# Folding step 1 of an FFT-style convolution over the sign of j and running it as four 64x64 TensorE tiles

## The chip, the cores and the metric

The kernel runs on one core of one Trainium2 chip. The metric is device time of one execution in microseconds, as the median of several runs. The engines are named as in the profile: PE (TensorE matmul), PEld (TensorE weight load), DVE (VectorE), ACT (ScalarE), POOL (GpSimd) and SP (SyncE, which issues nearly all DMAs here).

## The reference

Two layers follow each other. The first is a long convolution with a gate: a filter is made from position embeddings, the product x*v of 4 sequences of 11456 tokens and 128 channels is convolved with it through an FFT of twice the length, and the result is multiplied by x. The second is a soft mixture of experts over the 45824 resulting tokens. The change touches the first layer only.

```python
h_filt = (np.maximum(pos_emb @ w1, 0.0) @ w2) * np.exp(-0.01 * pos)[:, None]
u = x * v
Uf = np.fft.rfft(u, n=2 * S, axis=1)
Hf = np.fft.rfft(h_filt, n=2 * S, axis=0)
y = np.fft.irfft(Uf * Hf[None], n=2 * S, axis=1)[:, :S, :]
attn = x * y
logits = attn @ phi          # then softmax over tokens and over slots, 8 experts of
                             # 128 -> 1024 -> 128, and a weighted sum back to tokens
```

## The kernel before, in words

The transform has length 111 x 197, and a token's place is written as 111 j + r, with 105 values of j (from -52 to 52) and 56 of r, so that a long FFT becomes four short matrix steps. All data is fp32. Channels are worked in 8 groups g of 16 channels, so 64 (batch, channel) pairs in a group, and these in 16 units u of four pairs.

- **p1_load** (lines 197 to 218) fetches one unit: the tile `x` (line 199) and the tile `v` (line 209) from the queue of SP, multiplies them on POOL (line 211; every third unit of group 0 on DVE), and folds over the sign of r: `sd` is x(r)+x(-r) and x(r)-x(-r), two DVE instructions (line 214) of 112x256 each. `x` and `v` come from the pool `ld` of 5 buffers, which the tiles `xi` (the gate's x, lines 264 to 266) share; in group 0, `v` lies in an unused region instead. `sd` comes from the pool `st` of 3 buffers.
- **p1** (lines 220 to 222, `first` at lines 122 to 135) is step 1, the sum over j: for each of two pairs of channels two matmuls with 105 rows (j), 128 columns (both signs of r) and 198 moving columns (cosines and sines). One PSUM tile of pool `psa` (4 buffers) holds a pair of channels. Three ACT instructions take it out to `T` (lines 130, 131, 135; in group 0 the third is one of DVE, line 133).
- **p2** (lines 224 to 241) is the sum over r (line 229), the multiplication by the filter on DVE (line 234) and the complex sums on POOL (lines 240 and 241), which write `T` again.
- **p3** (lines 243 to 256) is the first inverse sum: four matmuls (line 247) for two pairs, one ACT copy `ec` (line 251) and two DVE instructions into `E` (line 253). PSUM pool `psb` has 4 buffers.
- **p4** (lines 269 to 289) is the last inverse sum (line 277) and the gate on DVE (line 283), and **p4_out** stores the tile `xo` (lines 301 and 309).

After the filter has been made, the main loop (lines 314 to 366) runs over g. In it come two stages. In the *mixed stage* each unit u issues p1_load for unit u+2, two p3 of group g-1, and p1 of unit u. In the *p2/p4 stage* p2 of group g and p4 of group g-1 alternate. Group 0 has p1 without p3, and then p2 with the filter's last step. Behind the loop follows the mixture of experts.

The order on each engine is made by a scheduler from this program order and its own estimates; `inorder` pins an instruction to the program's order. POOL's products of x and v are pinned. The DVE folds are pinned in group 1 only, and the `E` additions of group 0's p3 also. Each engine works its queue strictly in order, and SP its DMA issues too, so an entry that waits holds back all that stands behind it. A buffer of a pool is given to a new tile when the old tile's last reader has been placed; the DMA that fills it waits for that reader.

The built program gives the places of the tiles. In the mixed stages of groups 2 to 7 `v` of a unit takes the place of `v` of the unit two earlier, from unit 2 on, and the last reader of that one is the product on POOL (line 211); `x` takes the place of `x` three units earlier.

Of the kernel before, what the change touches and what calls it, by code (L numbers as in the profile page):

```python
# [59 lines left out]
def conv_part(ctx, tc, cp, moe, xf, vf, xi, pos, w1, w2, win, t1x, t1h, wt, t3, t4, hs, scr):  # L60
    nc = tc.nc
    ld = ctx.enter_context(tc.tile_pool(name="ld", bufs=5))
    st = ctx.enter_context(tc.tile_pool(name="st", bufs=3))
# [57 lines left out]

    def first(src, tab, dst, shift):

        ps = psa.tile([128, 2, 2, J], F32, tag="psa", name=f"p1_{next(ids)}")
        for i in range(2):
            nc.tensor.matmul(ps[:, i].rearrange("p s k -> p (s k)"), lhsT=src(i), rhs=tab,  # L126
                             start=True, stop=True)
# [2 lines left out]
        nc.scalar.activation(to[0:RP], pq[0:RP], AF.Copy)  # L130
# [66 lines left out]
    def p1_load(g, u):  # L197
        xt = ld.tile([JP, 4, 2 * RP], F32, tag="ld", name=f"x_{g}_{u}")
        dma = nc.sync.dma_start(out=xt, in_=xf[g, u])
        if g == 0:  # L200
# [8 lines left out]
        nc.sync.dma_start(out=vt, in_=vf[g, u])
# [1 line left out]
        inorder(eng.tensor_tensor(out=xt, in0=xt, in1=vt, op=ALU.mult))  # L211
        sd = st.tile([JP, 4, 2 * RP], F32, tag="st", name=f"sd_{g}_{u}")
        for h, op in ((0, ALU.add), (RP, ALU.subtract)):
            add = nc.vector.tensor_tensor(out=sd[:, :, h : h + RP], in0=xt[:, :, 0:RP], in1=xt[:, :, RP:],  # L214
                                          op=op)
# [575 lines left out]

def _layout(x, v, pos_emb):
    p, b, m = _index(ORG)

    def fold(a):
        t = np.stack([_take(a, p), _take(a, b, True)], 1)
        t = t.reshape(B, 2, JT, R, G, CG).transpose(4, 0, 5, 2, 1, 3)
        pad = np.zeros((G, C // 4, JP, 4, 2, RP), a.dtype)
        pad[:, :, :JT, :, :, :R] = t.reshape(G, C // 4, 4, JT, 2, R).transpose(0, 1, 3, 2, 4, 5)
        return pad.reshape(G, C // 4, JP, 4, 2 * RP)  # L800

# [53 lines left out]
```

## Time and profile before

| | |
|---|---|
| runs | 1116.45, 1119.45, 1120.04 us |
| median | 1119.45 us |
| profiled execution, span | 1116.5 us |
| PE / PEld busy | 1044.0 / 973.1 us |
| DVE / POOL / ACT busy | 860.3 / 591.4 / 567.5 us |
| p1 of group 0 | 70.5 to 99.9 us of the span |
| mixed stages, groups 1 to 7 | about 50 us each; the one of group 3 from 251.5 to 303.7 us |
| p2/p4 stage behind that | 303.7 to 351 us |

The page gives the profiled execution as its span only, and the span is as long as the fastest of the three runs (1116.45 us), 2.95 us under the median. In the profile a kernel matmul of fp32 stands as two MATMUL and two LDWEIGHTS instructions. Busy time of PE is that of the union of overlapping instructions, each with a fill and drain of about 0.16 us, so an engine that is "busy" may still have room. Durations of DVE and ACT instructions also overlap the next one's start a little, so what one costs in a row of equal ones is read from the distance of their starts, or from a merged row of several.

### The profile page before, as it was taken

How to read it: one execution, taken by the hardware profiler on the slowest of the kernel's cores; microseconds unless marked ns; L12 is line 12 of the kernel's file. 1: busy time of each engine (PE TensorE's matmuls, PEld its weight loads, DVE VectorE, ACT ScalarE, POOL GpSimd, SP SyncE). 2: the span in 40 equal slices, each digit the busy share in tenths (PEclk: the TensorE clock that was granted, in tenths of full speed). 3: DMA queues.
4: the chain of work that ended last, by engine and by line, in shares of the span. 5: the costliest groups of instructions: out<-in, count | busy, mean ns of one | idle time of the engine just before them, and what ended most of it. 6: DMA issues, size and time to landing. Idle time of an engine off the chain costs nothing.

```text
span 1116.5 us, 26150 instructions
## 1 busy us (share of the span) xinstructions
PE 1044.0 (94%) x9360; PEld 973.1 (87%) x9360; DVE 860.3 (77%) x1774; ACT 567.5 (51%) x1441; POOL 591.4 (53%) x742
## 2 busy tenths in 40 slices
PE   6998989999999999999999999999999979997997
PEld 6987989998999999899999999999999966664775
DVE  5237669786898779788868977787798649997797
ACT  0678559306901850491086039307801228775697
POOL 6203764484377437545743755474374006776874
PEclk9999989999999999999999999999999999998999
DMA  9614767246534834572474458247546698773388
GB/s 289 209 59 154 268 218 212 87 128 192 163 110 138 234 96 128 168 219 80 136 220 123 124 158 230 86 128 198 158 124 220 167 276 244 213 212 98 155 352 337
DMA packets 129484, 198.49 MB, mean 178 GB/s; under 512 B 15926, under 2 KB 71537, under 8 KB 129356
## 3 DMA queue, kind: packets, MB, share of 16 engines
q1 hardware_dynamic: 129070, 196.65, 57.6%
q8 instruction: 76, 1.25, 0.5%
q14 instruction: 52, 0.43, 0.1%
q10 hardware_dynamic: 254, 0.11, 0.0%
q0 software_dynamic: 32, 0.07, 0.0%
HBM read 136.88 MB, written 59.90 MB: 176 GB/s over the span
## 4 chain that ended last, share of the span: by engine, by line
PE 45%; DVE 15%; issue 11%; ACT 6%; DMA 5%; POOL 3%; SPq 1%; ACTq 0%; DVEq 0%; POOLq 0%
PE p L277 13%; PE p L229 10%; PE p L126 8%; PE p L247 8%; DVE E L253 5%; DMA v<-in_vf_dram 4%; PE ct L713 2%; POOL x L211 2%; DVE xreg L424 2%; ACT T L130 2%; PE pt L483 1%; DVE sd L214 1%; DVE rd L503 1%; DVE xreg L729 1%; ACT ec L251 1%
## 5 line engine op out<-in xcount | busy, mean ns | idle before, releaser
L251 ACT ACTIVATE ec<-p 99x224 f32<-99x224 f32 x256 | 83.8, 356 | 392.6 <-issue 336.8
L253 DVE TENSOR_TENSOR E<-p,ec 99x224 f32<-99x224 f32 x512 | 222.2, 552 | 46.3 <-ACT ec L251 45.8
L240 POOL TENSOR_TENSOR T<-m,m 111x256 f32<-111x256 f32 (+1 forms) x200 | 145.7, 729 | 185.1 <-DVE m L234 183.7
L234 DVE TENSOR_TENSOR m<-p,T 111x512 f32<-111x512 f32 (+1 forms) x350 | 215.7, 677 | 22.9 <-issue 16.6
L247 PE MATMUL p<-tab,T 111*99 111x112 f32 x2048 | 221.8, 262 | 7.1 <-POOL T L240 3.0
L211 POOL TENSOR_TENSOR x<-x,v 112x512 f32<-112x512 f32 x112 | 144.5, 1291 | 154.4 <-DMA v<-in_vf_dram 135.8
L247 PEld LDWEIGHTS p<-tab,T 111*99 111x99 f32 x2048 | 214.9, 171 | 12.1 <-POOL T L240 3.2
L277 PE MATMUL p<-E,tab 99*105 99x128 f32 (+1 forms) x1792 | 214.0, 275 | 11.4 <-DVE E L253 11.4
L277 PEld LDWEIGHTS p<-E,tab 99*105 99x105 f32 x1792 | 204.1, 173 | 13.7 <-DVE E L253 11.3
L126 PE MATMUL p<-tab1x,sd 105*128 105x198 f32 x1024 | 200.5, 341 | 14.5 <-DVE sd L214 11.7
L229 PE MATMUL p<-T,W 128*111 128x128 f32 x1584 | 200.0, 278 | 1.1 <-DVE T L133 1.1
L229 PEld LDWEIGHTS p<-T,W 128*111 128x111 f32 x1584 | 188.3, 175 | 2.8 <-DVE T L133 1.3
L126 PEld LDWEIGHTS p<-tab1x,sd 105*128 105x128 f32 x1024 | 171.1, 194 | 21.7 <-DVE sd L214 11.4
L214 DVE TENSOR_TENSOR sd<-x 112x256 f32<-112x256 f32 x256 | 116.4, 496 | 64.5 <-POOL x L211 54.6
L241 POOL TENSOR_TENSOR T<-m,m 111x256 f32<-111x256 f32 (+1 forms) x200 | 145.8, 729 | 0.0
L130 ACT ACTIVATE T<-p 64x396 f32<-64x396 f32 x256 | 136.9, 535 | 11.7 <-PE p L126 7.9
L283 DVE TENSOR_TENSOR xo<-p,xi 105x256 f32<-105x256 f32 x224 | 84.0, 416 | 43.8 <-PE p L277 33.4
L131 ACT ACTIVATE T<-p 64x198 f32<-64x198 f32 x256 | 90.1, 352 | 3.0
L135 ACT ACTIVATE T<-p 64x198 f32<-64x198 f32 x224 | 74.2, 331 | 0.0
L531 POOL TENSOR_TENSOR E<-lt,mx 128x480 f32<-128x480 f32 (+1 forms) x24 | 24.6, 1025 | 70.6 <-PE pt L483 67.5
L717 ACT ACTIVATE cs<-ct 96x512 fp32r<-96x512 f32 x96 | 53.3, 567 | 10.4 <-PE ct L713 7.1
L713 PE MATMUL ct<-ident,c 128*96 128x128 f32 x358 | 55.3, 274 | 2.2 <-POOL c L693 1.4
(95 smaller groups left out, 1065.6 us busy)
## 6 DMA issues: line engine op xcount, KB each, us to landing
x<-in_xf_dram SPq DMA_DIRECT2D x128, 224.0 KB
v<-in_vf_dram SPq DMA_DIRECT2D x112, 224.0 KB
xi<-in_xi_dram SPq DMA_DIRECT2D x112, 224.0 KB
out_dram<-xreg SPq DMA_DIRECT2D x22, 960.0 KB
xreg<-scr SPq DMA_DIRECT2D x21, 960.0 KB
scr<-xo SPq DMA_DIRECT2D x104, 192.0 KB
hs<-E SPq DMA_DIRECT2D x12, 1024.0 KB
T<-hs SPq DMA_DIRECT2D x63, 176.0 KB
```

Source lines behind the costliest of these rows:

```text
L126: nc.tensor.matmul(ps[:, i].rearrange("p s k -> p (s k)"), lhsT=src(i), rhs=tab, start=True, stop=True)
L130: nc.scalar.activation(to[0:RP], pq[0:RP], AF.Copy)
L211: inorder(eng.tensor_tensor(out=xt, in0=xt, in1=vt, op=ALU.mult))
L214: add = nc.vector.tensor_tensor(out=sd[:, :, h : h + RP], in0=xt[:, :, 0:RP], in1=xt[:, :, RP:], op=op)
L229: nc.tensor.matmul(ps[:, i].rearrange("p b c -> p (b c)"), lhsT=W[:, k0 + i, :], rhs=Tf[:, :, k0 + i, :], start=True, stop=True)
L234: nc.vector.tensor_mul(m[:, :n].rearrange("p k s c i -> p k (s c i)").rearrange("p k (b c) -> p k b c", c=CG), ps[:, :n], h[:, :, CG * s : ...
L240: nc.gpsimd.tensor_tensor(out=Ty[:, 0], in0=ms[0][:, :n, 0], in1=ms[1][:, :n, 1], op=ALU.subtract)
L241: nc.gpsimd.tensor_tensor(out=Ty[:, 1], in0=ms[1][:, :n, 0], in1=ms[0][:, :n, 1], op=ALU.add)
L247: nc.tensor.matmul(ps[:, i, 2 * s : 2 * s + 2, :].rearrange("p q r -> p (q r)"), lhsT=T[0:N1, s, c // CG, c % CG // 2, :, i], rhs=tab3[:, ...
L251: nc.scalar.activation(ec, ps[:, :, 2:4, :], AF.Copy)
L253: add = nc.vector.tensor_tensor(out=E[:J, :, 2 * s : 2 * s + 2, c : c + 2].rearrange("p r q c -> p c q r"), in0=ps[:, :, 0:2, :], in1=ec, ...
L277: nc.tensor.matmul(ps[:, i, :n], lhsT=tab4[:, s, o : o + JT], rhs=E[:J, r, s : s + 2 * n - 1 : 2, :], start=(s == 0), stop=(s == 1))
```

## The change

**Step 1 itself.** The sums over j and -j are folded too. The host lays x and v out with the 53 values of |j| on 64 partitions, for two channels at a time (partitions 0 to 63 and 64 to 127), and with four quarters along the free axis: the signs of j and of r. The two halves of j are added and subtracted first (`m`, new line 215: two instructions of 128x224, written over the tile `v`; on POOL, except in group 0, where half of them are on DVE). Then the two signs of r are added and subtracted as before (`d`, new line 219: two DVE instructions of 128x224, written over the tile `x`, read from `v`). The sums meet cosines and the differences meet sines, so that each output needs 53 rows, 64 columns and 99 moving columns: 16 matmuls a unit (new line 130), which cycle through the four 64x64 quarters of the array, in place of 4 of 105 rows, 128 columns and 198 moving columns. The two PSUM tiles of a unit each hold two channels in the order in which `T` wants them, and one ACT instruction of 128x396 takes each out (new line 135) in place of three.

**Around it.** `sd` has no buffer of its own any more. `ld` has 7 buffers instead of 5. p1 runs for two units at a time, in odd u, with the loads of the next two units behind them. A unit's x is 256 KB instead of 224 KB (rows of 64 for 56 values of r); v stays at 224 KB. The table `tab1x` is 128x297 instead of 105x198.

```diff
-    ld = ctx.enter_context(tc.tile_pool(name="ld", bufs=5))
+    ld = ctx.enter_context(tc.tile_pool(name="ld", bufs=7))
...
-    def first(src, tab, dst, shift):
+    def first(g, u, sd):
-        ps = psa.tile([128, 2, 2, J], F32, tag="psa", name=f"p1_{next(ids)}")
+        ps = [psa.tile([128, 2, 2, J], F32, tag="psa", name=f"p1_{g}_{u}_{h}") for h in range(2)]
         for i in range(2):
-            nc.tensor.matmul(ps[:, i].rearrange("p s k -> p (s k)"), lhsT=src(i), rhs=tab,
-                             start=True, stop=True)
-        to = dst.rearrange("p s k c -> p s c k")
-        pq = ps.rearrange("p c s k -> p s c k")
-        nc.scalar.activation(to[0:RP], pq[0:RP], AF.Copy)
-        nc.scalar.activation(to[RP:128, 0], pq[RP:128, 1], AF.Copy)
-        if shift:
-            nc.vector.tensor_scalar_mul(to[RP:128, 1], pq[RP:128, 0], -1.0)
-        else:
-            nc.scalar.activation(to[RP:128, 1], pq[RP:128, 0], AF.Copy, scale=-1.0)
+            for s in range(2):
+                for h in range(2):
+                    js = slice(RP * h, RP * h + JH)
+                    for d in range(2):
+                        nc.tensor.matmul(ps[h][RP * d : RP * d + RP, i, s, :], lhsT=sd[js, i, s, d, :],
+                                         rhs=tab1x[js, J * (s + d) : J * (s + d + 1)],
+                                         start=True, stop=True, tile_position=(RP * h, RP * d))
+        for h in range(2):
+            dst = T[:, :, u // 4, 2 * (u % 4) + h]
+            nc.scalar.activation(dst, ps[h].rearrange("p c s k -> p s k c"), AF.Copy)
...
         nc.sync.dma_start(out=vt, in_=vf[g, u])
         eng = nc.vector if g == 0 and u % 3 == 2 else nc.gpsimd
-        inorder(eng.tensor_tensor(out=xt, in0=xt, in1=vt, op=ALU.mult))
-        sd = st.tile([JP, 4, 2 * RP], F32, tag="st", name=f"sd_{g}_{u}")
-        for h, op in ((0, ALU.add), (RP, ALU.subtract)):
-            add = nc.vector.tensor_tensor(out=sd[:, :, h : h + RP], in0=xt[:, :, 0:RP], in1=xt[:, :, RP:],
+        inorder(eng.tensor_tensor(out=xr, in0=xr, in1=vt, op=ALU.mult))
+        for m, op in ((0, ALU.add), (2, ALU.subtract)):
+            eng = nc.vector if g == 0 and (u + m // 2) % 2 else nc.gpsimd
+            inorder(eng.tensor_tensor(out=vt[:, :, m : m + 2], in0=xr[:, :, 0:2], in1=xr[:, :, 2:4], op=op))
+        sd = xt.rearrange("p c (s d) r -> p c s d r", s=2)
+        vq = vt.rearrange("p c (s q) r -> p c s q r", s=2)
+        for d, op in ((0, ALU.add), (1, ALU.subtract)):
+            add = nc.vector.tensor_tensor(out=sd[:, :, :, d, :R], in0=vq[:, :, :, 0], in1=vq[:, :, :, 1],
                                           op=op)
...
-                if u + 2 < NU:
-                    sds[u + 2] = p1_load(g, u + 2)
                 if g > 0:
                     p3(g - 1, 4 * u)
                     p3(g - 1, 4 * u + 2)
-                p1(g, u, sds.pop(u))
+                if u % 2:
+                    p1(g, u - 1, sds.pop(u - 1))
+                    p1(g, u, sds.pop(u))
+                    for w in (u + 1, u + 2):
+                        if w < NU:
+                            sds[w] = p1_load(g, w)
```

**What the change does to the order.** First the queue of DVE in the mixed stage of group 3, before, from the fold of unit 10 on. `sd_3_10` is the fold of group 3's unit 10, and `E` the addition of two pairs of p3, as two instructions:

```order
L214 TENSOR_TENSOR sd_3_10_4057<-x_3_10_4052 112x4x64 x2
L253 TENSOR_TENSOR E_86<-p3_2_32_4060,ec_2_32_4065 99x2x2x56 x2
L253 TENSOR_TENSOR E_86<-p3_2_34_4069,ec_2_34_4074 99x2x2x56 x2
L214 TENSOR_TENSOR sd_3_11_4096<-x_3_11_4091 112x4x64 x2
L253 TENSOR_TENSOR E_86<-p3_2_36_4099,ec_2_36_4104 99x2x2x56 x2
L253 TENSOR_TENSOR E_86<-p3_2_38_4108,ec_2_38_4113 99x2x2x56 x2
L214 TENSOR_TENSOR sd_3_12_4135<-x_3_12_4130 112x4x64 x2
```

The same place after the change, where the fold over r writes `x` and reads `v`:

```order
L219 TENSOR_TENSOR x_3_10_4635<-v_3_10_4637 128x4x56
L257 TENSOR_TENSOR E_86<-p3_2_34_4567,ec_2_34_4572 99x2x2x56 x2
L257 TENSOR_TENSOR E_86<-p3_2_36_4577,ec_2_36_4582 99x2x2x56 x2
L257 TENSOR_TENSOR E_86<-p3_2_38_4586,ec_2_38_4591 99x2x2x56 x2
L219 TENSOR_TENSOR x_3_10_4635<-v_3_10_4637 128x4x56
L219 TENSOR_TENSOR x_3_11_4644<-v_3_11_4646 128x4x56 x2
L257 TENSOR_TENSOR E_86<-p3_2_40_4654,ec_2_40_4659 99x2x2x56 x2
L219 TENSOR_TENSOR x_3_12_4731<-v_3_12_4733 128x4x56
```

Before, one unit's two folds stand together and alternate with two pairs of additions. Now the first fold of an even unit stands three pairs of additions ahead of its second, and the odd unit's folds stand right behind that.

Now the queue of SP at the loads of units 11 to 13 of the same stage, before, with the semaphores for which each issue waits (the `DMAHW` ones are those of earlier DMAs; `T_85<-hs_57` is the load of the filter):

```order
L199 DMA x_3_11_4091<-in_xf_dram 112x512 [waits DVE_49]
L209 DMA v_3_11_4093<-in_vf_dram 112x512 [waits DMAHW7_49,DMAHW1_49,Pool_49]
L322 DMA T_85<-hs_57 128x352 [waits DMAHW0_49]
L199 DMA x_3_12_4130<-in_xf_dram 112x512 [waits DVE_49]
L209 DMA v_3_12_4132<-in_vf_dram 112x512 [waits DMAHW4_49,DMAHW2_49,Pool_49]
```

And after:

```order
L200 DMA x_3_11_4644<-in_xf_dram 128x512 [waits DMAHW6_49,PE_49]
L210 DMA v_3_11_4646<-in_vf_dram 128x448 [waits DMAHW1_49,DVE_49,Pool_49]
L326 DMA T_85<-hs_57 128x352 [waits DMAHW0_49]
L326 DMA T_85<-hs_57 128x352
L200 DMA x_3_12_4731<-in_xf_dram 128x512 [waits DMAHW2_49,PE_49]
L210 DMA v_3_12_4733<-in_vf_dram 128x448 [waits DMAHW3_49,DMAHW5_49,DVE_49,Pool_49]
```

The load of `v` waited for POOL alone, and now waits for DVE too. By the places in the built program, the same in groups 2 to 7, from unit 9 on `v` still takes the place of `v` two units earlier, whose last reader is now the second fold of line 219, and `x` that of `x` five units earlier, whose last reader is p1's matmul; up to unit 8 the seven places change hands between `x` and `v`. In group 1 `v` of odd units from 7 on does so as well, and both folds of both units of a pair stand together, ahead of four pairs of additions.

Last the queue of DVE at the head of the same stage. Before, the gate's products (`xo`) of the last p4 stand ahead of the first fold:

```order
L283 TENSOR_TENSOR xo0_2_6_3698<-p4_1_6_0_3700,xi0_1_6_3646 105x4x4x16
L283 TENSOR_TENSOR xo1_2_6_3699<-p4_1_6_0_3700,xi1_1_6_3648 105x4x4x16
L283 TENSOR_TENSOR xo0_2_6_3698<-p4_1_6_1_3711,xi0_1_6_3646 105x4x4x16
L283 TENSOR_TENSOR xo1_2_6_3699<-p4_1_6_1_3711,xi1_1_6_3648 105x4x4x16
L253 TENSOR_TENSOR E_86<-p3_2_0_3751,ec_2_0_3756 99x2x2x56
```

And after:

```order
L287 TENSOR_TENSOR xo0_2_6_4130<-p4_1_6_0_4132,xi0_1_6_4078 105x4x4x16
L287 TENSOR_TENSOR xo1_2_6_4131<-p4_1_6_0_4132,xi1_1_6_4080 105x4x4x16
L219 TENSOR_TENSOR x_3_0_4159<-v_3_0_4161 128x4x56
L287 TENSOR_TENSOR xo0_2_6_4130<-p4_1_6_1_4143,xi0_1_6_4078 105x4x4x16
L287 TENSOR_TENSOR xo1_2_6_4131<-p4_1_6_1_4143,xi1_1_6_4080 105x4x4x16
L219 TENSOR_TENSOR x_3_0_4159<-v_3_0_4161 128x4x56
```

The first fold of unit 0 now stands between the last products of the gate.

More of the change, by code (lines that the diff above doesn't have):

```diff
@@ L24 @@
 JP = 112
+JH = JT // 2 + 1
 R = 56
@@ L66, in conv_part @@
     psb = ctx.enter_context(tc.tile_pool(name="psb", bufs=4, space=bass.MemoryType.PSUM))
-    tab1x = cp.tile([JT, 2 * J], F32, tag="tab1x", name="tab1x")
+    tab1x = cp.tile([128, 3 * J], F32, tag="tab1x", name="tab1x")
     tab1h = cp.tile([J, 3 * J], F32, tag="tab1h", name="tab1h")
@@ L87, in conv_part @@
     NS = R // RB
-    ids = count()
     hid = moe.E[:J, : 2 * RP * FO].rearrange("p (s r f) -> p s r f", s=2, r=RP)
@@ L197, in p1_load @@
     def p1_load(g, u):
-        xt = ld.tile([JP, 4, 2 * RP], F32, tag="ld", name=f"x_{g}_{u}")
+        xt = ld.tile([128, 2, 4, RP], F32, tag="ld", name=f"x_{g}_{u}")
+        xr = xt[:, :, :, :R]
         dma = nc.sync.dma_start(out=xt, in_=xf[g, u])
@@ L202, in p1_load @@
         if g == 0:
-            k = 8 * RP * (u % 5)
-            vt = Hs[:JP].rearrange("p k x -> p (k x)")[:, k : k + 8 * RP]
-            vt = vt.rearrange("p (c r) -> p c r", c=4)
+            k = 8 * R * (u % 7)
+            vt = Hs.rearrange("p k x -> p (k x)")[:, k : k + 8 * R]
+            vt = vt.rearrange("p (c q r) -> p c q r", c=2, q=4)
         else:
-            vt = ld.tile([JP, 4, 2 * RP], F32, tag="ld", name=f"v_{g}_{u}")
+            vt = ld.tile([128, 2, 4, R], F32, tag="ld", name=f"v_{g}_{u}")
         nc.sync.dma_start(out=vt, in_=vf[g, u])
         eng = nc.vector if g == 0 and u % 3 == 2 else nc.gpsimd
-        inorder(eng.tensor_tensor(out=xt, in0=xt, in1=vt, op=ALU.mult))
-        sd = st.tile([JP, 4, 2 * RP], F32, tag="st", name=f"sd_{g}_{u}")
-        for h, op in ((0, ALU.add), (RP, ALU.subtract)):
-            add = nc.vector.tensor_tensor(out=sd[:, :, h : h + RP], in0=xt[:, :, 0:RP], in1=xt[:, :, RP:],
+        inorder(eng.tensor_tensor(out=xr, in0=xr, in1=vt, op=ALU.mult))
[6 more added lines that the diff above has]
+            add = nc.vector.tensor_tensor(out=sd[:, :, :, d, :R], in0=vq[:, :, :, 0], in1=vq[:, :, :, 1],
                                           op=op)
@@ L220, in p1 @@
     def p1(g, u, sd):
-        for h in range(0, 4, 2):
-            first(lambda i: sd[:JT, h + i, :], tab1x, T[:, :, u // 4, 2 * (u % 4) + h // 2], g == 0)
+        first(g, u, sd)
     def p2(g, k0):
@@ L740, in _constants @@
     f = np.float32
-    tj = np.arange(-(JT // 2), JT // 2 + 1)
     k2 = np.arange(J)
     r = np.arange(R)
-    g = 2 * np.pi * ((tj[:, None] * k2[None]) % N2) / N2
-    t1x = np.concatenate([np.cos(g), np.sin(g)], 1).astype(f)
+    g = 2 * np.pi * ((np.arange(JH)[:, None] * k2[None]) % N2) / N2
+    t1x = np.zeros((2, RP, 3 * J), f)
+    t1x[:, :JH] = np.concatenate([np.cos(g), np.sin(g), -np.cos(g)], 1)
+    t1x = t1x.reshape(2 * RP, 3 * J)
     g = 2 * np.pi * ((np.arange(J)[:, None] * k2[None]) % N2) / N2
@@ L793, in _layout, with fold @@
     p, b, m = _index(ORG)
[L795 to L800, printed above, removed]
+    def fold(a, w):
+        h = JT // 2
+        t = np.stack([_take(a, p)[:, h:], _take(a, b, True)[:, h:],
+                      _take(a, b, True)[:, h::-1], _take(a, p)[:, h::-1]], 1)
+        t[:, 2:, 0] = 0
+        t = t.reshape(B, 4, JH, R, G, CG // 4, 2, 2).transpose(4, 0, 5, 6, 2, 7, 1, 3)
+        pad = np.zeros((G, B, CG // 4, 2, RP, 2, 4, w), a.dtype)
+        pad[:, :, :, :, :JH, :, :, :R] = t
+        return pad.reshape(G, C // 4, 2 * RP, 2, 4, w)
     t = np.stack([_take(x, p), _take(x, m)], 0)
@@ L807, in _layout @@
     pe = pe.reshape(2, J, R // 4, 4, FO).transpose(2, 0, 4, 3, 1).reshape(R // 4, 128, 4, J)
-    return fold(x), fold(v), xi, np.ascontiguousarray(pe)
+    return fold(x, RP), fold(v, R), xi, np.ascontiguousarray(pe)
 def _rows():
```

## The prediction

> **What bounds the kernel now.** I read the page first, for the balance of the engines:
>
> ```profile
> PE 1044.0 (94%) x9360; PEld 973.1 (87%) x9360; DVE 860.3 (77%) x1774; ACT 567.5 (51%) x1441; POOL 591.4 (53%) x742
> ```
>
> TensorE looks like the bound, and step 1 is part of its work. But this is an average over stages. The sums by stretch give the p1 of group 0, the mixed stage of group 3 and the p2/p4 stage behind it:
>
> ```profile
> core 0: us, PE busy (x) PEld busy (x) DVE busy (x) ACT busy (x) POOL busy (x), PEclk, DMA share, GB/s
> 70.50:99.90 29.40, 25.46 (x142) 21.29 (x141) 25.14 (x58) 26.36 (x61) 6.47 (x5) 1.00 0.45 134
> 251.50:303.70 52.20, 49.39 (x386) 48.22 (x384) 40.28 (x94) 42.19 (x122) 21.01 (x17) 0.97 0.67 190
> 303.70:351.00 47.30, 45.97 (x412) 45.95 (x412) 41.11 (x78) 2.29 (x7) 33.00 (x48) 1.00 0.38 110
> ```
>
> Only the first two kinds hold step 1, so only they can change: the 29.4 us of group 0 and seven mixed stages of about 50 us. In the settled half of a mixed stage the chain of waits is all PE:
>
> ```profile
> 286.38 1.53 PE p L247 x16
> 287.91 1.36 PE p L126 x8
> 289.27 1.53 PE p L247 x16
> 290.80 1.36 PE p L126 x8
> ```
>
> One unit is 2.89 us: 1.53 of p3 and 1.36 of p1. Yet the same view over the whole run has loads of `v` standing in the chain; three of the mixed stage of group 4:
>
> ```profile
> 365.55 3.22 DMA v<-in_vf_dram
> 370.23 4.60 DMA v<-in_vf_dram
> 376.30 3.67 DMA v<-in_vf_dram
> ```
>
> So the loading runs close to PE. Its loop is read in time order; the rows are of SP, POOL and DVE:
>
> ```profile
> 284.58 1.28 POOL L211 TENSOR_TENSOR x<-x,v 112x512 f32<-112x512 f32 x1 [2.13 <-DVE sd L214]
> 285.88 0.31 SPq L209 DMA_DIRECT2D v<-in_vf_dram  x1
> 288.74 0.31 SPq L209 DMA_DIRECT2D v<-in_vf_dram  x1
> 289.75 1.77 DVE L253 TENSOR_TENSOR E<-p,ec 99x224 f32<-99x224 f32 x4 [0.25 <-ACT ec L251]
> 289.87 1.29 POOL L211 TENSOR_TENSOR x<-x,v 112x512 f32<-112x512 f32 x1 [1.16 <-DMA v<-in_vf_dram]
> 291.18 0.31 SPq L209 DMA_DIRECT2D v<-in_vf_dram  x1
> 291.37 0.73 DVE L214 TENSOR_TENSOR sd<-x 112x256 f32<-112x256 f32 x2
> 292.94 2.51 POOL L211 TENSOR_TENSOR x<-x,v 112x512 f32<-112x512 f32 x2 [1.79 <-DMA v<-in_vf_dram]
> ```
>
> The product of unit 11 ends at 285.86, and 0.02 us later the load of `v` of unit 13 goes out into the freed place; its product starts at 289.87, 3.99 us after. The loop of two units is thus 289.87 - 284.58 = 5.29 us, against 2 x 2.89 = 5.78 of PE: half a microsecond of slack. From issue to product the three loads take 3.99, 4.20 (288.74 to 292.94) and 3.0 us (291.18 to the second of the two products, 1.25 us after 292.94).
>
> **The change part by part.**
>
> *PE.* p1 has 32 instructions a unit of 99 columns in place of 8 of 198. Rows with tiles, of the timeline of PE:
>
> ```profile
> 120.01 2.00 PE L164 MATMUL fl<-w2s,E 64*111 64x128 f32 x32
> 121.94 0.82 PE L229 MATMUL p<-T,W 128*111 128x128 f32 x5
> 953.24 1.07 PE L560 MATMUL pa<-xreg,ev 128*32 128x128 f32 x30
> ```
>
> Whole matmuls take 1.36/8 = 0.170 us for 198 columns. Two row tiles take (121.94 - 120.01)/32 = 0.060 us each for 128 columns, about half of 0.170 x 128/198 = 0.110; four column tiles take 1.07/30 = 0.036 with the drain in it. So tiles do run side by side. Four quarters of 99 columns take 0.170 x 99/198 = 0.085 us, and 32 instructions 0.68 us, with the drain at each switch some 0.75. Per unit PE falls to 1.53 + 0.75 = 2.3 us.
>
> *ACT.* Three copies for a pair of channels become one, of a form that the trace has:
>
> ```profile
> L146 ACT ACTIVATE T<-f 128x396 f32<-128x396 f32 x32 | 16.6, 518 | 28.6 <-PE f L143 28.4
> L130 ACT ACTIVATE T<-p 64x396 f32<-64x396 f32 x256 | 136.9, 535 | 11.7 <-PE p L126 7.9
> ```
>
> The first stands for the new one and costs what line 130 costs alone, so lines 131 and 135 go. Both gains, PE's and ACT's, are worth nothing where something else is late.
>
> *POOL and DVE.* The prices:
>
> ```profile
> L211 POOL TENSOR_TENSOR x<-x,v 112x512 f32<-112x512 f32 x112 | 144.5, 1291 | 154.4 <-DMA v<-in_vf_dram 135.8 <-DVE E L253 8.9 <-DVE sd L214 8.1
> L240 POOL TENSOR_TENSOR T<-m,m 111x256 f32<-111x256 f32 x192 | 140.9, 734 | 184.9 <-DVE m L234 183.4 <-PE fl L164 1.4
> L240 POOL TENSOR_TENSOR T<-m,m 111x192 f32<-111x192 f32 x8 | 4.8, 605 | 0.3 <-DVE m L234 0.3
> ```
>
> The product shrinks to 448 elements: 1.29 x 448/512 = 1.13 us. The two new instructions have 224 elements, between 192 at 0.605 and 256 at 0.734: 0.67 each. POOL goes from 1.29 to 2.47 us a unit. DVE's two folds take 0.73 for 256 elements each, so 0.64 for 224. Four additions to `E` take 291.37 - 289.75 = 1.62 us until the next fold starts, 0.40 each.
>
> POOL and the folds also exclude each other:
>
> ```profile
> 260.88 1.26 POOL L211 TENSOR_TENSOR x<-x,v 112x512 f32<-112x512 f32 x1 [0.53 <-DVE E L253]
> 261.01 1.75 DVE L214 TENSOR_TENSOR sd<-x 112x256 f32<-112x256 f32 x2
> ```
>
> These two folds take 1.75 us instead of 0.73: the first lasts until POOL has ended. The additions to `E`, which run beside POOL at 289.87, show nothing of it. The Trainium skill (SBUF — State Buffer, Who interferes with whom) states it as a rule: a DVE instruction with two SBUF inputs and a GpSimd instruction that reads SBUF block each other fully. By that rule, the trace agreeing, the two engines share one port and a unit needs the sum of both. From the rows above that sum is 2.47 + 0.64 = 3.1 us a unit, over PE's old 2.89, where it was 1.29 + 0.73 = 2.0.
>
> *The loop of the loads.* In groups 2 to 7, from unit 9 on, `v` still takes the place of `v` two units earlier, but that place is free only after the second fold over r. For an even unit three pairs of `E` additions stand between its two folds on DVE, and all of them queue behind a fold that waits for POOL. Pair by pair, from second fold to second fold: issue 0.02; load to product 3.6 (the middle of 3.0 to 4.2); POOL 2.47; first fold 0.32; six additions 2.4; wait for POOL's port, which is then busy with the odd unit, 0.45 (half of an instruction of 0.67 to 1.13); second fold 0.32. Sum 9.6 us, in place of 5.78. The last three pairs (units 10 to 15) so cost 3 x 3.8 = 11.5 us more a stage. Bounds: 3.0 for the load and no port wait give 8.5 (+8 a stage); 4.2 and a wait for whole products on both folds give 12 (+19).
>
> *Units 4 to 9.* The seven places still hold; the port binds, with 3.1 us and some handing over, say 3.3: 6 x 0.41 = 2.5 us (0 to 6).
>
> *Head of the stage.* The first fold of unit 0 now stands ahead of the last gate products, and SP's stores and the load of `v` of unit 2 behind these:
>
> ```profile
> 251.90 1.30 POOL L211 TENSOR_TENSOR x<-x,v 112x512 f32<-112x512 f32 x1
> 252.11 1.46 SPq L301 DMA_DIRECT2D scr<-xo  x4
> 254.80 0.37 SPq L209 DMA_DIRECT2D v<-in_vf_dram  x1
> ```
>
> POOL's first unit would end at 251.90 + 2.47 = 254.4 and the stores come some 2.9 us later than 252.1. Against that, `v` of unit 1 is on its way earlier, since seven places let it pass. I take +1.4 us (-2 to 3).
>
> *Sum.* A stage of groups 2 to 7: 11.5 + 2.5 + 1.4 = 15.4 us; six of them 92. Group 1 has another order (both folds together, ahead of the additions) and the same loop for odd units: 3.6 + 2.47 + 0.64 + 0.45 = 7.2 a pair instead of 5.78, over seven pairs +10 (0 to 15). Group 0: ACT and PE get faster, POOL and DVE dearer by 1.2 us a unit, which the seven `ld` buffers let run ahead; I take 0 (-6 to 6). The 32 KB more of each `x` have their price within the load's 3.0 to 4.2 us. Together +102 us.
>
> The span of 1116.5 becomes 1218.5. The median of the runs lies 2.95 above that execution, so I say 1222 us.
>
> **The rivals.**
>
> *The loads stay hidden* (faster). If the scheduler's distances suffice and a pair's loop stays under 5.78 us, POOL's 2.47 bounds the mixed stage: 16 x (2.89 - 2.47) = 6.7 us less, seven times 47, 1072 us. For it speak the 154.4 us that POOL idled before line 211; against it that these were waits for exactly this loop, which grows by all that is named above. Were PE still the bound there, with its 2.3 us, it would be 16 x 0.59 x 7 = 66 us less, 1053. The Trainium skill (TensorEngine Tiling (Array Packing), Overview) speaks for this one: it names four independent tiles of 64x64, and up to twice the throughput for each dimension of at most 64.
>
> *Only the port binds* (slower, less). If DVE never holds a pair's loop up, each unit costs 3.1 to 3.3 instead of 2.89: 16 x 0.3 = 4.8 us a stage, 34 in seven, 1153 us.
>
> *The quarters do not run side by side.* Then p1 takes 32 x 0.085 = 2.7 us instead of 1.36, 16 x 1.36 x 8 = 174 us more, 1293. Line 164's spacing speaks against it.
>
> **How the numbers follow.** A change under 0.3% (3.4 us) can't be told from none here. Forecast 0.79; port alone 0.11; loads hidden 0.06; quarters in a row 0.02; gains and losses that cancel 0.02. The forecast's own terms reach from 6 x (8 + 0 - 2) + 0 - 6 = +30 to 6 x 28 + 21 = +190 with all ends at once. Eight in ten is less: I let the loop's pair go from 8.7 to 11 us and the rest stay near its middle, which gives 6 x 12.6 to 6 x 19.6 and 10, +86 to +128; with some room for the small terms +80 to +140, and down to the port alone. Range 1152 to 1260. Slower 0.92, faster 0.06, the same 0.02.
>
> **What would show it.** Right: in groups 2 to 7 p1 instructions of some 0.02 us each; loads of `v` of units 10, 12 and 14 some 9 to 10 us apart; the chain of waits there made of the load, POOL and DVE, with PE idle; folds with means well over 0.42 us. Wrong: product after product on POOL without waits, or PE still filling the mixed stages, or a stage under 52 us.

## The result, and the profile after

The changed kernel takes 1205.1 us (median; 1197.0 to 1206.07, 4 runs) against 1117.95 us (1115.3 to 1120.04, 4 runs): 1.076 times as long, 95% interval 1.072 to 1.080. Its profiled execution has a span of 1203.2 us, 86.7 more than before.

The balance of the engines on the page, after:

```profile
PE 1041.6 (87%) x12432; PEld 952.5 (79%) x12432; DVE 885.0 (74%) x1758; ACT 405.0 (34%) x961; POOL 742.3 (62%) x982
```

ACT is 162 us lighter, POOL 151 us heavier, and TensorE, with less to do, is not less busy. The sums by stretch, for the same three places as before (the prediction, and the table ahead of it, count the groups one too high here: the stage that began at 251.50 is that of group 2, and the three loads from 365.55 on belong to group 3):

```profile
core 0: us, PE busy (x) PEld busy (x) DVE busy (x) ACT busy (x) POOL busy (x), PEclk, DMA share, GB/s
71.20:98.80 27.60, 21.35 (x503) 17.94 (x502) 16.31 (x30) 13.52 (x31) 13.86 (x15) 0.67 0.49 152
261.70:324.50 62.80, 47.09 (x770) 43.57 (x768) 41.66 (x93) 21.05 (x58) 40.19 (x49) 0.89 0.48 149
324.50:373.50 49.00, 47.36 (x434) 47.15 (x425) 42.71 (x82) 2.28 (x6) 34.23 (x50) 1.00 0.44 133
```

Most of the loss here is in the mixed stage: 62.80 us instead of 52.20, with 15.7 us of it in which TensorE does nothing. In the settled half of the next one (group 3) the chain of waits, all PE before, reads:

```profile
408.20 4.11 DMA v<-in_vf_dram
...
412.48 1.12 POOL x L212
...
414.98 1.30 DVE x L219
416.28 1.41 DVE E L257 x4
417.69 0.05 issue
417.74 0.94 DVE E L257 x2
418.68 0.23 DVE x L219
418.91 0.02 SPq L210
418.93 0.37 issue
419.31 2.49 DMA v<-in_vf_dram
421.79 0.02 issue
421.82 0.04 POOLq L212
421.86 0.08 issue
421.94 0.02 POOLq L215
421.96 1.15 POOL x L212
423.11 0.07 issue
423.17 1.28 POOL v L215 x2
```

A load of `v`, the product, POOL's two new instructions (between 412.48 and 414.98), the first fold, six additions to `E`, the second fold, and only then the next load of `v`. Product to product, 412.48 to 421.96, is 9.48 us. What SyncE waited for with its loads of `v`, before and after, in the mixed stage of group 3 (us in total, times, longest):

```profile
SPq L209 <- POOL x L211: 12.1, 11, 1.5
```
```profile
SPq L210 <- DVE x L219: 21.7, 6, 6.8
```

The releaser has changed from POOL's product to DVE's fold, and the longest wait from 1.5 to 6.8 us. The timeline shows what that does to TensorE, in brackets at the end of its row:

```profile
414.98 1.30 DVE L219 TENSOR_TENSOR x<-v 128x224 f32<-128x224 f32 x1 [4.13 <-POOL v L215]
416.20 2.48 DVE L257 TENSOR_TENSOR E<-p,ec 99x224 f32<-99x224 f32 x6
417.26 4.66 PE L251 MATMUL p<-tab,T 111*99 111x112 f32 x24 [5.28 <-DVE E L257]
```

DVE stands 4.13 us at a fold whose data is still on its way; the additions behind it, ready long since, keep p3's PSUM; TensorE idles 5.28 us, and then goes on at half clock (24 instructions in 4.66 us, where 16 took 1.53 before).

The table holds means over the mixed stages of groups 2 to 7, worked out from the starts of the products (POOL's rows of the timeline, units counted from 0) and of p3; "middle" is a third of the way from unit 2 to unit 8, "tail" a third of that from unit 8 to unit 14, so each is the time of a pair of units. "Period" is from one group's first p3 to the next one's, "half clock" the time of a stage's p3 in which the granted clock is 0.5. A ratio is to runs of the kernel before that were taken along with that kernel (their medians lie between 1117.95 and 1120.64 us). In number 3 one of four runs (1177.48 us) was in a slower state of the chip, and its median is that of the other three.

| kernel | median us | ratio to before (95%) | first pair | middle | tail | p3 first to last | period | half clock |
|---|---|---|---|---|---|---|---|---|
| before | 1117.95 | | 7.25 | 5.73 | 5.10 | 49.5 | 100.3 | 1.1 |
| after | 1205.1 | 1.076 (1.072-1.080) | 9.12 | 5.93 | 9.45 | 63.7 | 113.3 | 17.7 |
| 1 own tile | 1157.0 | 1.037 (1.033-1.040) | 5.53 | 5.60 | 7.24 | 56.1 | 105.9 | 13.0 |
| 2 nine places | 1153.9 | 1.033 (1.030-1.036) | 5.27 | 6.04 | 7.32 | 59.4 | 108.3 | 18.8 |
| 3 pinned | 1162.3 | 1.040 (1.035-1.045) | 5.18 | 6.64 | 7.10 | 54.1 | 107.1 | 10.2 |
| 4 no fold over j | 1113.3 | 0.996 (0.993-0.999) | 5.63 | 6.02 | 7.34 | 51.5 | 101.3 | 7.9 |
| 5 nine, pinned | 1090.5 | 0.975 (0.973-0.978) | 5.09 | 5.69 | 5.92 | 47.2 | 97.0 | 6.8 |
| 6 p1 twice | 1350.6 | 1.208 (1.205-1.210) | 9.24 | 7.13 | 13.29 | 86.9 | 137.4 | 31.2 |
| 7 unit by unit | 1203.2 | 1.076 (1.073-1.079) | 9.13 | 6.28 | 7.76 | 65.0 | 113.6 | 20.5 |
| 8 half on DVE | 1154.1 | 1.032 (1.029-1.035) | 3.91 | 6.06 | 7.65 | 55.3 | 105.3 | 13.1 |
| 9 own tile, pinned | 1147.7 | 1.024 (1.020-1.028) | 5.53 | 5.64 | 7.25 | 49.6 | 104.1 | 7.4 |
| 10 before, nine, pinned | 1109.6 | 0.990 (0.987-0.994) | 2.45 | 5.36 | 4.95 | 49.2 | 98.5 | 2.8 |
| 11 all three | 1095.9 | 0.979 (0.975-0.983) | 5.52 | 5.74 | 5.74 | 46.9 | 97.8 | 6.3 |
| 12 nine, pinned, no fold | 1011.9 | 0.903 (0.900-0.907) | 2.19 | 5.05 | 4.44 | 37.7 | 86.6 | 0.0 |

### The profile page after: what moved, and what is told of

Read it like the earlier page. It is cut to its first block, busy times and chain, and to the rows that moved or that the text cites. A ratio compares the mean times of both kernels' runs of the same rounds, so it can differ in the third digit from the quotient of the medians.

```text
span 1203.2 us, 32107 instructions
## 1 busy us (share of the span) xinstructions
PE 1041.6 (87%) x12432; PEld 952.5 (79%) x12432; DVE 885.0 (74%) x1758; ACT 405.0 (34%) x961; POOL 742.3 (62%) x982
## 4 chain that ended last, share of the span: by engine, by line
PE 33%; DVE 20%; POOL 11%; DMA 11%; issue 10%; SPq 1%; ACT 1%; POOLq 0%; DVEq 0%; ACTq 0%
PE p L281 11%; PE p L233 11%; DMA v<-in_vf_dram 8%; DVE E L257 8%; POOL v L215 5%; POOL x L212 4%; DVE x L219 4%; PE p L251 3%; PE ct L720 2%; PE p L130 2%; PE pt L490 1%; DVE rd L510 1%; DVE xreg L431 1%; DVE xreg L736 1%; DVE ev L557 1%
## 5 line engine op out<-in xcount | busy, mean ns | idle before, releaser
L251 PE MATMUL p<-tab,T 111*99 111x112 f32 x2048 | 260.9, 292 | 86.6 <-DVE E L257 69.4
L251 PEld LDWEIGHTS p<-tab,T 111*99 111x99 f32 x2048 | 243.7, 195 | 100.8 <-issue 90.0
L255 ACT ACTIVATE ec<-p 99x224 f32<-99x224 f32 x256 | 89.4, 367 | 623.4 <-issue 337.3
L219 DVE TENSOR_TENSOR x<-v 128x224 f32<-128x224 f32 x224 | 130.3, 618 | 136.9 <-POOL v L215 136.8
L212 POOL TENSOR_TENSOR x<-x,v 128x448 f32<-128x448 f32 x112 | 132.2, 1181 | 127.8 <-DMA v<-in_vf_dram 96.7
L130 PE MATMUL p<-tab1x,x 53*64 53x99 f32 x4096 | 136.0, 276 | 31.9 <-issue 17.1
L215 POOL TENSOR_TENSOR v<-x 128x224 f32<-128x224 f32 x224 | 152.8, 702 | 8.8
L130 PEld LDWEIGHTS p<-tab1x,x 53*64 53x64 f32 x4096 | 113.9, 152 | 49.3 <-issue 19.1
L135 ACT ACTIVATE T<-p 128x396 f32<-128x396 f32 x256 | 108.5, 507 | 32.4 <-PE p L130 31.9
L720 PE MATMUL ct<-ident,c 128*96 128x128 f32 x358 | 55.3, 274 | 2.2 <-POOL c L700 1.4
L490 PE MATMUL pt<-ident,xreg 128*128 128x128 f32 x358 | 49.9, 283 | 6.6 <-DVE xreg L431 3.7
```

Source lines behind the costliest of these rows:

```text
L130: nc.tensor.matmul(ps[h][RP * d : RP * d + RP, i, s, :], lhsT=sd[js, i, s, d, :], rhs=tab1x[js, J * (s + d) : J * (s + d + 1)], start=True ...
L135: nc.scalar.activation(dst, ps[h].rearrange("p c s k -> p s k c"), AF.Copy)
L212: inorder(eng.tensor_tensor(out=xr, in0=xr, in1=vt, op=ALU.mult))
L215: inorder(eng.tensor_tensor(out=vt[:, :, m : m + 2], in0=xr[:, :, 0:2], in1=xr[:, :, 2:4], op=op))
L219: add = nc.vector.tensor_tensor(out=sd[:, :, :, d, :R], in0=vq[:, :, :, 0], in1=vq[:, :, :, 1], op=op)
L251: nc.tensor.matmul(ps[:, i, 2 * s : 2 * s + 2, :].rearrange("p q r -> p (q r)"), lhsT=T[0:N1, s, c // CG, c % CG // 2, :, i], rhs=tab3[:, ...
```

## The experiments

All are edits of the changed kernel, but for the tenth. Numbers 4 and 12 leave out a part of the computation.

**1: the fold over the sign of j in a tile of its own.**

```diff
+        mt = st.tile([128, 2, 4, R], F32, tag="st", name=f"m_{g}_{u}")
-            inorder(eng.tensor_tensor(out=vt[:, :, m : m + 2], in0=xr[:, :, 0:2], in1=xr[:, :, 2:4], op=op))
+            inorder(eng.tensor_tensor(out=mt[:, :, m : m + 2], in0=xr[:, :, 0:2], in1=xr[:, :, 2:4], op=op))
+        vt = mt
```

> The fold over the sign of j writes a tile of its own (from the three st buffers) in place of the tile of v; nothing else changes, the same instructions with the same durations. The place of v is then free after POOL's last instruction, as in the kernel before, and no longer after DVE's second fold. Theory (the loop of the loads runs through DVE): a pair of units takes issue 0.02 + load 3.6 + POOL 2.47 = 6.1 us, so the port sum of 6.2 to 6.6 us binds instead of 9.6: some 3 us less for each of the last three pairs, 9 a stage, 54 in six stages: about 1150 us (1135 to 1165). Rival (the two POOL instructions and the shared port set the time, wherever the place comes free): within 15 us of the changed kernel, 1190 to 1205.

1157.0 us, 48 less than the changed kernel, as the theory had it and far from the rival. The size is right in part by luck: in the tail a pair takes 7.24 us and not 6.2 to 6.6, so that gives 6.6 us a stage instead of 9, and the first pair gives another 3.6 that the expectation hadn't counted. At the end of a stage `v` turns round in one place here, as in number 9: in that of group 4 the products start at 509.64, 513.38, 517.48 and 521.61, and each of the three loads between them goes out 0.02 us after a product has ended.

**2: nine places.**

```diff
-    ld = ctx.enter_context(tc.tile_pool(name="ld", bufs=7))
+    ld = ctx.enter_context(tc.tile_pool(name="ld", bufs=9))
...
```

The lines that move four small tables into `E` are left out here; they come with nine places in every experiment.

> Nine ld buffers in place of seven (small tables of the filter stage move into an unused part of E to make room). Theory (places): v then takes a place freed about one unit earlier, three units of way instead of two, so a unit costs at most 9.6/3 = 3.2 us instead of 4.8, near the port sum: 1.5 us less for each of the last six units, 9 a stage, about 1150 us (1130 to 1170). Rival (port and POOL time): the buffers change nothing in the settled part, 1190 to 1205.

1153.9 us. The tail falls from 9.45 to 7.32, again not all the way, while the first pair loses 3.9 us; some 6 us of the gain are ahead of group 1, whose p3 starts at 146.9 instead of 152.9.

**3: both folds over r pinned.**

```diff
-            if g == 1:
+            if g:
                 inorder(add)
```

> The two folds over r are kept in program order in groups 2 to 7 too, as group 1 has them, so that no E additions stand between the two folds of a unit. Theory (the order on DVE lengthens the loop): the pair costs 7.2 us instead of 9.6, three pairs a stage, 7 us a stage and 43 in all: about 1162 us (1145 to 1180); the mixed stages become as long as that of group 1 (54.7 us against a mean of 64). Rival (port and POOL time, or the places alone): 1190 to 1210.

1162.3 us against 1162 expected; the tail is 7.10 where 7.2 was worked out, and the stages are as long as group 1's. The p2/p4 stage behind them became some 3 us longer (period less p3: 53.0 against 49.6), which wasn't followed up.

**4: no fold over the sign of j.**

```diff
-        inorder(eng.tensor_tensor(out=xr, in0=xr, in1=vt, op=ALU.mult))
-        for m, op in ((0, ALU.add), (2, ALU.subtract)):
-            eng = nc.vector if g == 0 and (u + m // 2) % 2 else nc.gpsimd
-            inorder(eng.tensor_tensor(out=vt[:, :, m : m + 2], in0=xr[:, :, 0:2], in1=xr[:, :, 2:4], op=op))
+        inorder(eng.tensor_tensor(out=vt, in0=xr, in1=vt, op=ALU.mult))
```

> Leaves out part of the computation: the fold over the sign of j (the two POOL instructions of 224 elements) is not done; the product goes into the tile of v straight away, everything else stays. It gives the price of these two instructions. Theory (loop): a pair loses the 1.34 us of the even unit's two instructions and some port wait, 9.6 becomes 7.9 to 8.2, still above the 5.78 of the kernel before, while the units ahead of it go at TensorE's 2.3 us: about +3 us a stage against before, 1115 to 1150. Rival (POOL's time and the port alone made the loss): nothing holds TensorE up any more, 16 x 0.59 us less a mixed stage, 1050 to 1075.

1113.3 us: just under the theory's range, and 38 above the rival's. A tail pair is shorter than expected too, 7.34 us for 7.9 to 8.2. The page's first line:

```profile
PE 1000.3 (90%) x12432; PEld 918.4 (83%) x12432; DVE 835.6 (75%) x1742; ACT 402.1 (36%) x961; POOL 577.5 (52%) x742
```

POOL is 165 us lighter than in the changed kernel, and lighter than before the change (591.4); still nothing is gained in a mixed stage, whose period is 101.3 against 100.3 before (the gain is in group 0: p3 of the next group starts 7.6 us earlier). SyncE's waits with `v`, in the stage of group 4, are like those of the changed kernel:

```profile
SPq L210 <- DVE x L216: 20.7, 6, 5.1
```

So the way through DVE holds the loads with or without POOL's two instructions, and these lengthen it: a tail pair takes 7.34 us with them gone, 9.45 with them.

**5: nine places and pinned** (the edits of 2 and 3).

> Nine ld buffers and the folds over r pinned in groups 2 to 7: both of the edits that gained by themselves. Theory (places and the order on DVE are two holds of one loop): with both gone the units follow each other as POOL and the port allow, 2.6 to 3.1 us (2.6 is the distance of products in the first ten units with nine places), 42 to 50 us a mixed stage with 3 us of head, like the 49 of the kernel before: 1105 to 1140 us. Rival (something else, such as TensorE's half clock or the pairing of units, keeps the stage long): the gains do not add, 1145 to 1165.

1090.5 us: faster than the kernel before by 2.5%, and better than the theory's range. Each cure alone left 7.1 to 7.3 us in the tail; both together 5.92. Now POOL hardly waits (the page has 5.9 us of idling ahead of its products, for 127.8 in the changed kernel); the sums of the mixed stage of group 4 (columns as above):

```profile
438.29:488.10 49.81, 44.64 (x770) 40.95 (x768) 45.69 (x98) 21.53 (x62) 43.59 (x49) 0.93 0.67 199
```

POOL, DVE and TensorE are all at about 90%. The timeline shows how POOL and the folds exclude each other now:

```profile
467.13 1.13 POOL L214 TENSOR_TENSOR x<-x,v 128x448 f32<-128x448 f32 x1
467.20 2.07 DVE L221 TENSOR_TENSOR x<-v 128x224 f32<-128x224 f32 x2 [0.55 <-POOL v L217]
...
472.22 2.47 POOL L214 TENSOR_TENSOR x<-x,v 128x448 f32<-128x448 f32 x1
472.40 1.28 DVE L221 TENSOR_TENSOR x<-v 128x224 f32<-128x224 f32 x4
```

At 467 POOL runs its full pace and two folds take 2.07 us; at 472 four folds in a row take 0.32 each, and the product, whose row begins 0.18 us ahead of theirs, lasts 2.47 instead of 1.13.

**6: each matmul of step 1 twice.**

```diff
-                        nc.tensor.matmul(ps[h][RP * d : RP * d + RP, i, s, :], lhsT=sd[js, i, s, d, :],
-                                         rhs=tab1x[js, J * (s + d) : J * (s + d + 1)],
-                                         start=True, stop=True, tile_position=(RP * h, RP * d))
+                        for _ in range(2):
+                            nc.tensor.matmul(ps[h][RP * d : RP * d + RP, i, s, :], lhsT=sd[js, i, s, d, :],
+                                             rhs=tab1x[js, J * (s + d) : J * (s + d + 1)],
+                                             start=True, stop=True, tile_position=(RP * h, RP * d))
```

> The changed kernel with each of the 32 matmuls of a unit of step 1 issued twice (the second writes the same values over the first), so TensorE has some 0.7 us a unit more to do and idles less. Theory (the loads hold the mixed stages and TensorE has time to spare there; its half clock only follows from the idling): within 15 us of the changed kernel, 1190 to 1220. Rival one (the half clock is a cause of its own, about 28 pieces of 3.4 to 6.8 us at half speed): the fuller TensorE keeps its clock and the time falls to 1150 to 1185. Rival two (TensorE is on the path): 16 x 0.7 x 8 = 90 us more, about 1290.

1350.6 us: none of the three, and nearest to the rival that has TensorE on the path (1290). Groups on the page:

```profile
L252 PE MATMUL p<-tab,T 111*99 111x112 f32 x2048 | 268.1, 297 | 135.8 <-DVE E L258 118.8
L220 DVE TENSOR_TENSOR x<-v 128x224 f32<-128x224 f32 x224 | 111.4, 526 | 303.1 <-POOL v L216 302.9
L131 PE MATMUL p<-tab1x,x 53*64 53x99 f32 x8192 | 245.5, 273 | 19.7 <-issue 16.1
```

Step 1 costs TensorE 110 us more (245.5 against 136.0), but DVE also waits 303 us for POOL ahead of its folds (137 in the changed kernel), and p3 waits 119 us for additions to `E` (69 in the changed kernel). The scheduler has made another order on DVE: in the tail of the stage of group 4 two folds stand together, then six additions, a fold, two additions and a fold. Two things changed at once, so this says nothing on the half clock, and the claim that TensorE has time to spare isn't borne out by it either. Nor does it price the order on DVE: how much of the 145 us is TensorE's and how much the order's isn't shown.

**7: unit by unit.** The loop over units as the kernel before has it (loads of unit u + 2, p3, p1 of unit u).

> The order of the kernel before: the loads of unit u + 2 ahead of p3 and p1 of unit u, one unit at a time, in place of the pairs; seven ld buffers, folds not pinned. Theory (the pairing only matters through the additions between the folds): the way of the two-unit loop keeps load 3.6, POOL 2.47, folds 0.64, and some 1.6 of E additions and 0.45 of port wait, 8.8 us instead of 9.6: 2.4 us a stage, about 1190 us (1165 to 1205). Rival (issuing the loads in pairs is what makes the loop long): the loss goes to the port's share alone, 1140 to 1160.

1203.2 us, at the upper end of the theory's range and no different from the changed kernel. The pairing is not the cause. The tail's 7.76 us are given back in the last unit: from unit 10 to unit 15 it is 21.1 us against 21.7 with pairs.

**8: half of the fold over j on DVE,** on top of number 5.

```diff
-            eng = nc.vector if g == 0 and (u + m // 2) % 2 else nc.gpsimd
+            eng = nc.vector if (m if g else (u + m // 2) % 2) else nc.gpsimd
```

> Nine buffers, pinned, and the second of the two instructions of the fold over the sign of j on DVE instead of POOL in groups 1 to 7. POOL has 1.13 + 0.67 = 1.8 us a unit, DVE 1.6 of additions and 0.95 of folds; the sum on the port goes from 3.1 to 2.76. Theory (with the loop gone, POOL's time and the port are what is left): 0.3 us a unit or 5 us a stage less than nine buffers and pinning alone, 25 to 35 us in all, 1075 to 1110. Rival (DVE, which waits in order, or the half clock is what is left): no faster than that kernel, or slower by up to 20.

1154.1 us, 64 more than number 5, where the theory had 25 to 35 less; even the rival's 20 is passed. The sums of the mixed stage of group 4:

```profile
468.10:524.00 55.90, 48.55 (x706) 43.98 (x704) 53.12 (x107) 20.91 (x58) 31.94 (x33) 0.85 0.57 166
```

DVE is busy for 95% of it and has become the bound, while POOL idles 24 us of 55.9. The instruction moved costs DVE nearly as much as POOL, 631 ns for 705. Its shortest one lasts 362 ns, so the mean holds time in which it waits for POOL's instructions in turn:

```profile
L217 POOL TENSOR_TENSOR v<-x 128x224 f32<-128x224 f32 x112 | 78.9, 705 | 8.8
L217 DVE TENSOR_TENSOR v<-x 128x224 f32<-128x224 f32 x112 | 70.7, 631 | 6.4 <-POOL x L214 6.4
L221 DVE TENSOR_TENSOR x<-v 128x224 f32<-128x224 f32 x224 | 147.8, 699 | 11.8 <-DVE v L217 1.4 <-POOL v L217 0.6
```

DVE's 53.1 us over 16 units are 3.3 us a unit, where the theory had counted 1.6 + 0.95 = 2.55.

**9: own tile and pinned, seven places** (the edits of 1 and 3).

> Seven ld buffers as in the changed kernel, the fold over the sign of j into a tile of its own, and the folds over r pinned in groups 2 to 7. Theory (two holds, the place of v that DVE frees and the order on DVE): both are gone here as well as with nine places and pinning, so 1085 to 1115 us. Rival (the place of x, held from its load until step 1 has read the folded values, is a hold of its own that nine places removed and this does not): 1120 to 1160.

1147.7 us: the rival's number. DVE is out of the way of `v`, and the tail stays at 7.25. p3 from first to last is as short as before the change (49.6), but step 1's last instruction starts 52.8 us after the first p3, for 50.8 before, and what follows up to the next p3 takes 51.3, for 49.5. So half of the 3.8 us a period lies in the p2/p4 stage, as in number 3, and its cause stays open. Its chain of waits in the stage of group 4:

```profile
507.45 1.15 POOL x L212
508.60 0.02 issue
508.62 2.51 DMA v<-in_vf_dram
511.13 0.02 issue
...
511.27 1.14 POOL x L212
512.41 0.02 issue
512.42 2.35 DMA v<-in_vf_dram
...
514.94 1.15 POOL x L212
```

A product ends, 0.02 us later the next unit's `v` goes out, and its product starts when that has landed: 3.67 to 3.82 us a unit, with POOL idle in between. `v` turns round in one place here. That the tiles of `x`, which live until step 1 has read them, take the other places is the reading that fits; the rows show the turn, not the owners of the rest.

**10: the kernel before, nine places and pinned.**

> The kernel before with nine ld buffers (small tables moved into E) and its folds over r pinned in all groups: the two cures without the change. Theory (TensorE bounds the mixed stages of the kernel before, its loop of loads has half a microsecond to spare): little to gain there, 1105 to 1120 us, some of it in group 0. Rival (the gain of 28 us comes from buffers and order, and the change has no part in it): 1085 to 1100.

1109.6 us, as the theory said: 0.990 of the kernel before, where the same cures take the changed kernel to 0.975 of it. Its products run further ahead (first pair 2.45 us instead of 7.25), but p3 from first to last takes 49.2 us as it did: TensorE bounds it, busy for 47.24 of the 49.70 us from 453.3 to 503 in the stage of group 4. So of number 5's 2.5% (28 us) 1.0% would be had without the change, by buffers and order, and 1.5%, some 17 us, belong to it.

**11: all three cures.**

> Nine buffers, pinned, and the fold over the sign of j into a tile of its own: all three cures. Theory (POOL's 2.47 us a unit and the folds that wait for it are what is left, a load of v stands in the chain for some 3 us once or twice a stage): 1 to 2 us a stage less at most, 1075 to 1092 us. Rival (the three st buffers that the fold then takes from the stores hold up the stage's ends): 1092 to 1110.

1095.9 us, in the rival's range and not in the theory's; the intervals of 11 and 5 overlap, so nothing is gained over nine places and pinning. Whether the three `st` buffers are the reason, as the rival had it, wasn't looked at.

**12: number 5 without the fold over j.**

> Nine buffers, pinned, and the fold over the sign of j left out (part of the computation: the product goes into the tile of v, the two POOL instructions are gone). Theory (with places and order cured, POOL's 2.47 us a unit is what keeps the stage at 47 us): POOL falls to 1.13 a unit, TensorE's 2.3 us bind, 16 x 2.3 + 3 = 40 us a stage, 1035 to 1055 us. Rival (TensorE, ACT and DVE wait for each other in turn, p3's PSUM for the E additions above all): 44 us or more a stage, 1065 to 1090.

1011.9 us, even below the theory's range; 7.4 us of it are ahead of group 1, whose p3 starts at 140.2 instead of number 5's 147.6. The sums of the mixed stage of group 4:

```profile
401.45:440.70 39.25, 38.87 (x770) 36.71 (x768) 38.39 (x97) 22.08 (x62) 21.09 (x17) 1.00 0.82 253
```

TensorE is busy for 99% of 39.25 us, 2.45 a unit. With places and order cured, the fold over j costs 1090.5 - 1011.9 = 79 us.

## Why the prediction was right, step by step

**The mechanism was the one forecast**: the loop of the loads got longer than TensorE's unit, and TensorE waits. Its signs came: in the stage of group 3 the products of units 10, 12 and 14 are 9.5 and 9.3 us apart, and the folds last 0.62 us in the mean.

*The loop's pair*: 9.6 us worked out, 9.45 measured (tail), against 5.10 before, where 5.78 was taken. Of its parts one holds as worked out: taking DVE's additions out from between the folds gave 7.10, for 7.2. The others are right in direction and off in size: taking POOL's two instructions out gave 7.34, for 7.9 to 8.2, and freeing `v` ahead of DVE 7.24, for 6.2 to 6.6.

*PE*: 0.68 to 0.75 us a unit was right at full clock, or just under (in number 5 a pair's 64 instructions start at 473.63 and the next p3 at 475.16, 1.53 us later, so 0.77 a unit and 0.024 an instruction; the rival of quarters in a row, with 0.085 each, is out). Over the run it is 136.0/128 = 1.06. Most of the rest is the half clock, which no step had foreseen: 892 of the 4096 instructions start under it and make up 47.7 of the 136.0 us, and number 12, which has none under it, is busy for 106.8 with the same instructions.

```profile
L130 PE MATMUL p<-tab1x,x 53*64 53x99 f32 x4096 | 136.0, 276 | 31.9 <-issue 17.1 <-ACT T L135 8.9 <-DVE x L219 5.7
L215 POOL TENSOR_TENSOR v<-x 128x224 f32<-128x224 f32 x224 | 152.8, 702 | 8.8
L212 POOL TENSOR_TENSOR x<-x,v 128x448 f32<-128x448 f32 x112 | 132.2, 1181 | 127.8 <-DMA v<-in_vf_dram 96.7 <-DVE E L257 13.6 <-PE p L251 7.8
L135 ACT ACTIVATE T<-p 128x396 f32<-128x396 f32 x256 | 108.5, 507 | 32.4 <-PE p L130 31.9
```

*POOL*: 1.18 + 2 x 0.70 = 2.58 us a unit, for 2.47. *ACT*: 507 ns a copy, for 518.

*Units 4 to 9* is the term that was mis-sized most: 3.3 us a unit for the port would be 6.6 a pair, and 5.93 was measured, 0.2 over the kernel before. Where POOL idles only once, for 0.65 us (number 5, from 438.72 to 481.28 in its stage of group 4) fifteen products are 42.56/15 = 2.84 us apart, not 3.1: part of the folds' 0.64 us finds POOL between two instructions. *Head*: +1.4 said; the first pair takes 9.12 instead of 7.25, +1.9.

*The sum*: a period of groups 2 to 7 grew by 13.0 us, not 15.4 (p3 by 14.2; the stage behind it became 1.1 shorter). Six of them make 78.3, group 1 +10.7 (for +10), group 0 -0.5 (for 0), the rest -1.8: 86.7 in place of 102. All but two of the missing 15 us are the six stages. By the products, though, the three terms come to 15.5 a stage, for 15.4: 13.0 from the tail (3 x 4.35, for 11.5), 0.6 from the middle (for 2.5) and 1.9 from the head (for 1.4). That their sum fits so well is luck, as the misses cancel. What it lacks is two gains, 1.3 us a stage in p3 outside these three terms and 1.1 us behind p3.

*The rivals.* "The loads stay hidden" is what the change gives once its loop is cured: number 5's 1090.5 lies near the 1072 worked out from POOL's 2.47, some 11 us of the distance to the kernel before being the cures' own (number 10). The Trainium skill (TensorEngine Tiling (Array Packing), Overview) speaks of four independent tiles of 64x64. That step 1 as such tiles gains once nothing stands in its way is what number 12 shows, 1011.9, though it leaves the fold out and has ACT's shorter copies and both cures in it. "Only the port binds" gave 1153, as a loss of 34 us; with the loop cured the port's bound is a gain of 28 instead, as 2.84 us a unit is under the old 2.89 and group 0 ends 6 us earlier.

What was missed is that two holds lie in the same loop, either of which alone keeps a tail pair at 7.1 to 7.3 us: the places (1, 2 and 9 change these) and the order on DVE (3). Both together are dear by themselves: in number 4, POOL was nearly as free as before the change, and the mixed stages still gained nothing.

## What to carry to other kernels

A stage that one engine seems to fill can have a loop of buffers right beneath it; before making that engine faster, add up the whole way from a place's release to its next release, with every instruction that stands between on an engine that works in order. When a load waits, ask which instruction frees its place and what that one is queued behind: here more places and a fixed order of two folds turned 7.6% slower into 2.5% faster, and either of them alone did not. An instruction moved to relieve one engine of a shared port can cost the other one nearly as much (number 8).
